# A state-space layer and a long-convolution layer on one core: a new order of all operations, planned with the DMA engines as one shared server, and larger blocks for x, q and the output

## The chip, the core and the metric

The kernel runs on one core of one Trainium2 chip. The metric is the device time of one execution in microseconds (us), lower is better. An execution varies: the kernel before took 229.8 to 240.2 us in its first three runs. A run more than 1.5% above the fastest of the same kernel in the same set is called slow and left out of ratios. A ratio here is the mean time of one kernel's fast runs over the mean time of the other kernel's fast runs in the same rounds on the same chip, so it is not quite the ratio of the medians that are quoted beside it.

## The reference, cut to what matters

Two layers read different inputs and fill the two halves of one output, 2048 x 1280.

```python
def _A_ref(x, Lambda_re, Lambda_im, B_re, B_im, C_re, C_im, log_dt, Dskip):   # x: 1 x 2048 x 640
    Lam_bar = jnp.exp(jnp.exp(log_dt) * Lam)
    Bu = einsum("bld,pd->blp", x, ((Lam_bar - 1.0) / Lam)[:, None] * Bmat)
    for t in range(L): h = Lam_bar * h + Bu[:, t, :]       # linear recurrence, 640 complex states
    y = 2.0 * einsum("blp,dp->bld", hseq, Cmat).real + x * Dskip

def _B_ref(q, k, v, shift_k, ssm_k, ssm_D):                # 1 x 2048 x 640 each
    kv = (k convolved with 4 taps shift_k) * v
    y = irfft(rfft(kv padded) * rfft(ssm_k padded)) + kv * ssm_D   # convolution of length 2048
    return q * y

return concatenate([a, b], axis=-1)
```

The kernel turns both into matmuls: the recurrence is done in blocks, the long convolution as a Fourier transform in two steps (`s1`, `s2`, the product, inverse steps `i2`, `i1`), for five groups of 128 channels.

## The kernel before: what the change and the argument touch

About 720 operations are declared with what they read and write. A text, ORDER, lists them by name, with the engine as a suffix where there is a choice (A ScalarE, D VectorE, G GpSimd, S SyncE). The kernel walks through the list and puts each operation on its engine's queue. Each engine does its queue strictly in order, so **the order decides what an engine waits for**.

```python
ORDER = """
ld_ldt ld_lre J0 consts J1 nrow ld_lim nrowf w0 xna pidx Dm0 w1 Dm1/G xnb hst1/S c4 B00 w2 bc zero par mk E0 ...
... zt2 s1h31 st_32/G e1h30/A ... d01_9 i120 cm30 ... py0_02 ob20 ...
... zt4 py1_21 i110 ey_21/D i131 ob10 ...
"""                                                       # cut: the rest of 720 names

def f_nrow():                                             # the seven powers of the sets, one iota each
    for i, n in enumerate(self.set_n):
        g.iota(nrow[:, i, :], pattern=[[0, 10]], base=n, channel_multiplier=0)

# the filter of group G, 512 KB (hst), and ssm_D (Dm), about 1 KB; dtap adds D to the filter's tap 0
op(f"hst{G}", {"SP": 0.4, "POOL": 1.2}, lambda e: self.eng[e].dma_start(
    out=self.S4(st)[:, 0:2048].rearrange("p (b t) -> p b t", b=16),
    in_=self.B_ssm_k[c0:c0 + 128, :].rearrange("(b c) (a t) -> (c a) b t", c=8, t=128)), ...)
op(f"dtap{G}", {"POOL": 0.2, "DVE": 0.1}, lambda e: self.eng[e].tensor_tensor(
    out=self.S4(st)[:, 0:2048:128], in0=self.S4(st)[:, 0:2048:128], in1=self.Dm[:, 16 * G:16 * G + 16], op=ALU.add), ...)

# B is loaded by four transposing loads from SyncE (B00, B01, B10, B11)
nc.sync.dma_start_transpose(out=self.BT[:, :, u, 320 * h:320 * h + 320], in_=ap[320 * h:320 * h + 320, :].rearrange(...))

# between the inverse steps: 1 MB from SBUF to SBUF, transposed (zt); i1 then reads Zt
op(f"zt{G}", {"SP": 5.0}, lambda e: nc.sync.dma_start_transpose(
    out=self.S8(Zt)[:].rearrange("p (b n) -> p b n", b=32), in_=self.S8(Zs)[:].rearrange("p (b n) -> p b n", b=32)), ...)
```

## Time and profile before

| | before |
|---|---|
| median of 3 runs | 232.91 us (229.82 to 240.19) |
| profiled span, TensorE busy | 230.8, 195.7 |
| TensorE idle | 35.1 |
| VectorE, ScalarE, GpSimd busy | 180.8, 140.7, 44.1 |

The span runs from the first to the last instruction. Where TensorE is the bound, what an order can win is TensorE's idle time plus what a throttled clock costs; the prediction below shows the lines and adds them up stage by stage.

### The profile page before, as it was taken

How to read it: one execution, taken by the hardware profiler on the slowest of the kernel's cores; microseconds unless marked ns; L12 is line 12 of the kernel's file. 1: busy time of each engine (PE TensorE's matmuls, PEld its weight loads, DVE VectorE, ACT ScalarE, POOL GpSimd, SP SyncE). 2: the span in 40 equal slices, each digit the busy share in tenths (PEclk: the TensorE clock that was granted, in tenths of full speed). 3: DMA queues.
4: the chain of work that ended last, by engine and by line, in shares of the span. 5: the costliest groups of instructions: out<-in, count | busy, mean ns of one | idle time of the engine just before them, and what ended most of it. 6: DMA issues, size and time to landing. Idle time of an engine off the chain costs nothing. (4 is left out here: it accounts for less than half of the span.)

```text
span 230.8 us, 8736 instructions
## 1 busy us (share of the span) xinstructions
PE 195.7 (85%) x3947; PEld 137.3 (59%) x3947; DVE 180.8 (78%) x279; ACT 140.7 (61%) x166; POOL 44.1 (19%) x67
## 2 busy tenths in 40 slices
PE   0619996979999999997659999659999999999953
PEld 0507443657456665645458776346777877777752
DVE  7699999859958799997546999915779899965641
ACT  3846928958556998778526795704267677852000
POOL 8288441600000020210200001002220003001600
PEclk9976999999999999999988999958999999999999
DMA  5999998997723079699968019990895482339966
GB/s 169 188 224 200 167 189 192 169 164 156 86 94 91 6 163 89 136 218 217 254 108 159 0 55 211 193 181 29 163 158 138 148 185 60 100 81 188 235 164 119
DMA packets 85407, 33.74 MB, mean 146 GB/s; under 512 B 81466, under 2 KB 82746, under 8 KB 85370
## 3 DMA queue, kind: packets, MB, share of 16 engines
q1 hardware_dynamic: 82972, 25.37, 61.0%
q0 software_dynamic: 2368, 7.81, 15.1%
q8 instruction: 30, 0.49, 0.9%
q14 instruction: 7, 0.06, 0.1%
q10 hardware_dynamic: 30, 0.00, 0.0%
HBM read 9.19 MB, written 7.86 MB: 74 GB/s over the span
## 5 line engine op out<-in xcount | busy, mean ns | idle before, releaser
L331 ACT CAST s<-ps 128x1024 bf16<-128x1024 f32 x81 | 78.4, 1020 | 26.0 <-PE ps L1002 12.9
L751 PE MATMUL ps<-xT,BC 128*64 128x512 bf16 x400 | 47.4, 381 | 0.2 <-ACT s L331 0.2
L899 PE MATMUL ps<-BC,hb 128*128 128x320 bf16 x240 | 38.1, 307 | 1.9 <-issue 1.7
L751 PEld LDWEIGHTS <-BC 128*64 128x64 bf16 x400 | 21.5, 110 | 18.0 <-issue 2.0
L1002 PE MATMUL ps<-R,s 64*64 64x128 bf16 x1280 | 24.7, 234 | 8.4 <-DVE s L924 4.3
L899 PEld LDWEIGHTS <-hb 128*128 128x128 bf16 x240 | 22.6, 100 | 12.4 <-issue 2.4
L1002 PEld LDWEIGHTS <-s 64*64 64x64 bf16 x1280 | 21.5, 118 | 13.0 <-issue 6.5
L333 DVE CAST s<-ps 128x1024 bf16<-128x1024 f32 x19 | 22.8, 1220 | 6.0 <-PE ps L1002 4.4
L856 DVE TENSOR_TENSOR hb<-ps,hb 128x512 bf16<-128x512 f32 x30 | 19.6, 684 | 9.3 <-PE ps L852 9.3
L1061 DVE TENSOR_TENSOR s<-s,s 128x1024 bf16<-128x1024 bf16 (+1 forms) x30 | 25.2, 866 | 1.0 <-PE ps L1002 0.3
L331 ACT CAST yo<-ps 128x640 bf16<-128x640 f32 x11 | 7.6, 691 | 28.8 <-PE ps L903 19.3
L1038 PE MATMUL ps<-s,Wre 128*64 128x128 bf16 x320 | 21.1, 221 | 0.4 <-issue 0.2
L1038 PE MATMUL ps<-s,Wim 128*64 128x128 bf16 x320 | 20.7, 219 | 0.0
L977 DVE TENSOR_TENSOR s<-s,s 128x2048 bf16<-128x2048 bf16 x15 | 19.3, 1290 | 1.2 <-ACT s L969 0.8
L1132 PE MATMUL ps<-Ct,s 128*64 128x64 bf16 x640 | 12.6, 201 | 8.8 <-DMA s<-s 6.9
L1038 PEld LDWEIGHTS <-Wre 128*64 128x64 bf16 x320 | 18.0, 110 | 2.8 <-issue 1.2
L1139 DVE TENSOR_TENSOR s<-ps,s 128x1024 bf16<-128x1024 f32 x10 | 12.1, 1222 | 9.0 <-PE ps L1132 6.6
L1038 PEld LDWEIGHTS <-Wim 128*64 128x64 bf16 x320 | 18.1, 110 | 0.9 <-issue 0.4
L331 ACT CAST hb<-ps 128x768 bf16<-128x768 f32 x17 | 13.5, 798 | 8.0 <-PE ps L751 8.0
L1132 PEld LDWEIGHTS <-s 128*64 128x64 bf16 x640 | 11.7, 117 | 10.1 <-DMA s<-s 7.6
L912 POOL DMA_DIRECT2D out_dram<-yo x6 | 3.4, 573 | 72.5 <-ACT yo L331 37.3
L1061 DVE TENSOR_TENSOR s<-s 128x1024 bf16<-128x1024 bf16 x20 | 13.8, 688 | 0.3
(161 smaller groups left out, 296.3 us busy)
## 6 DMA issues: line engine op xcount, KB each, us to landing
kvd<-s SPq DMA_DIRECT2D x4, 512.0 KB, 3.3
out_dram<-yo SPq DMA_DIRECT2D x10, 160.0 KB, 4.5
s<-in_B_ssm_k_dram POOLq DMA_DIRECT2D x3, 512.0 KB, 6.5
s<-kvd POOLq DMA_DIRECT2D x3, 512.0 KB, 7.6
s<-in_B_q_dram POOLq DMA_DIRECT2D x6, 256.0 KB, 8.0
out_dram<-s POOLq DMA_DIRECT2D x6, 256.0 KB, 5.6
s<-in_B_ssm_k_dram SPq DMA_DIRECT2D x2, 512.0 KB, 7.0
s<-kvd SPq DMA_DIRECT2D x2, 512.0 KB, 4.8
```

Of the source, the lines that this page charges most:

```text
L331: self.nc.scalar.copy(out=out, in_=in_)
L333: self.eng[e].tensor_copy(out=out, in_=in_)
L751: nc.tensor.matmul(P[64 * ri:64 * ri + 64, b, :], lhsT=self.BT[:, k, ri, 64 * j:64 * j + 64], rhs=self.xT[:, k, hf, 2 * b:2 * b + 2, :].re ...
L856: v.tensor_tensor(out=hv(r), in0=self.P(p2)[:, 0, :].rearrange("p (h m) -> p h m", h=2), in1=hv(r), op=ALU.add)
L899: nc.tensor.matmul(P[:, part, 0:320], lhsT=hap(j), rhs=self.CT[:, j, c0:c0 + 320], start=(j == 0), stop=False)
L912: self.eng[e].dma_start(out=self.o2[r0:r0 + 2033:16, 0:D], in_=self.yo[yo.slot][:])
L977: op(f"ca{j}{G}{h}", {"DVE": dve_tt(W_)}, lambda e, c=c, tt=tt: v.tensor_tensor(out=c(), in0=c(), in1=tt(), op=ALU.add), r=[f"tm{G}{h}"], ...
L1002: nc.tensor.matmul(P[64 * ri:64 * ri + 64, r, 128 * b4:128 * b4 + 128], lhsT=d[64 * r:64 * r + 64, 4 * qd + b4, a0, :], rhs=self.R[64 * r: ...
L1038: nc.tensor.matmul(P[64 * pi:64 * pi + 64, ri, 128 * k4:128 * k4 + 128], lhsT=W[:, kp, pi, :], rhs=A[:, kp + 16 * pi, :], start=True, stop ...
L1061: v.tensor_tensor(out=o, in0=a, in1=b, op=op_)
L1132: nc.tensor.matmul(P[64 * ah:64 * ah + 64, b // 8, 64 * (b % 8):64 * (b % 8) + 64], lhsT=Z[:, 16 * h + b, 64 * ri:64 * ri + 64], rhs=self. ...
L1139: v.tensor_tensor(out=o, in0=self.P(pt)[:].rearrange("p s (b a c) -> p a (s b) c", b=8, a=16), in1=o, op=ALU.mult)
```

## The change

**Intent.** The program that had found the old order counted a transposing load as time of SyncE and almost none of the DMA engines'; the new one lets it take its turn in the one server that all transfers share, and counts GpSimd work of 0.25 us or more as a slowdown of VectorE beside it. These model constants run on no engine. What runs is different in these ways:

- the order is new throughout, and most stores and loads are issued by SyncE instead of GpSimd;
- the first half of x arrives in two pieces of 640 KB, not 960 and 320, and is transposed and copied by piece;
- q and the output of the second layer move as one transfer of 128-row blocks each, not two of 64-row blocks (the columns of Ct, the matrix of the last inverse step, are reordered to match);
- the second product of the spectrum (pQ) is one operation with a reversed block view instead of two;
- `nrow` is filled by two iotas instead of seven, and one small copy (F16) is gone.

```diff
-ld_ldt ld_lre J0 consts J1 nrow ld_lim nrowf w0 xna pidx Dm0 w1 Dm1/G xnb hst1/S c4 B00 w2 bc zero par mk E0 ld_sk/G p0 dtb R
+xn0 ld_lre J0 consts nrow xn1 J1 zero ld_ldt E0 pidx w0 ld_lim c4 nrowf hst1/G B00 E1 wi0 kz0/D bc kz1/G px00 wm0 px02 ex00/A
+px04 Dm0 w1 ex02/A Dm1/G px10 ex04/A par px12 ex10/A px14 p0 ex14/D B01 dtb ex12/A p1 fi w2 nrho ph mk rn k0 R dtap1/G Ct
 ... (the rest of the order is replaced as well)
-            for i, n in enumerate(self.set_n):
-                g.iota(nrow[:, i, :], pattern=[[0, 10]], base=n, channel_multiplier=0)
+            g.iota(nrow[:, 0:3, :], pattern=[[1, 3], [0, 10]], base=1, channel_multiplier=0)
+            g.iota(nrow[:, 3:7, :], pattern=[[4, 4], [0, 10]], base=4, channel_multiplier=0)
 ...
-        op("xna", ... in_=xr[:, 0:6, :]) ; op("xnb", ... in_=xr[:, 6:8, :])          # 960 KB, 320 KB
+        for b in range(2): op(f"xn{b}", ... in_=xs[:, 0, b])                          # 640 KB each
 ...
-                    tt(X(0), X(0), H(1), ALU.mult)
-                    tt(X(1), X(1), H(0), ALU.mult)
+                    o = self.S4(xs)[:, 0:2048].rearrange("p (r n) -> p r n", r=2)
+                    tt(o, o, self.S8(Hf)[:, 2048 * h:2048 * h + 2048].rearrange("p (r n) -> p r n", r=2)[:, ::-1, :], ALU.mult)
 ...
-            for hh in range(2):
-                self.eng[e].dma_start(out=self.S4(q)[64 * hh:64 * hh + 64, 0:2048]..., in_=q2[1024 * hh:1024 * hh + 1024, c0:c0 + 128]...)
+        self.eng[e].dma_start(out=self.S4(q)[:, 0:2048].rearrange("p (a c) -> p a c", a=16),
+                              in_=q2[:, c0:c0 + 128].rearrange("(a p) c -> p a c", p=128))
```

## The prediction

> **What bounds the kernel now.** I read the page first (busy time, the 40 slices), then busy time by stage, cut at the points where TensorE stops and starts, then the waits of TensorE, the chain that ended last, and the order of time in the first 26 us.
>
> ```profile
> PE 195.7 (85%) x3947; PEld 137.3 (59%) x3947; DVE 180.8 (78%) x279; ACT 140.7 (61%) x166; POOL 44.1 (19%) x67
> ...
> PE   0619996979999999997659999659999999999953
> ...
> PEclk9976999999999999999988999958999999999999
> DMA  5999998997723079699968019990895482339966
> ```
>
> TensorE is the bound wherever it has work. The figures to look at are the low digits of the PE row: the start, slices 18 to 21, slices 25 and 26, the end. The clock row drops just after each.
>
> ```profile
> 0.00:17.33 17.33, 4.77 (x43) 4.00 (x43) 13.84 (x50) 10.09 (x16) 11.29 (x29) 0.91 0.99 194
> ...
> 36.25:50.00 13.75, 10.67 (x276) 7.54 (x276) 11.58 (x32) 11.91 (x15) 4.97 (x6) 1.00 1.01 180
> ...
> 100.00:121.00 21.00, 14.43 (x472) 10.42 (x474) 13.66 (x22) 13.07 (x19) 2.13 (x3) 0.97 1.07 200
> ...
> 140.00:152.30 12.30, 7.60 (x164) 4.76 (x161) 9.42 (x13) 6.34 (x6) 0.95 (x3) 0.93 1.27 178
> ...
> 205.00:227.20 22.20, 19.22 (x481) 15.27 (x479) 9.91 (x10) 3.63 (x4) 4.48 (x6) 1.00 0.92 189
> 227.20:230.80 3.60, 0.00 (x0) 0.00 (x0) 0.82 (x1) 0.00 (x0) 0.00 (x0) 1.00 0.39 88
> ```
>
> Columns: stretch, length, busy PE, PEld, DVE, ACT, POOL, clock, DMA share, GB/s. Length less PE busy is TensorE's idle time: 12.56, 3.08, 6.57, 4.70, 2.98 and 3.60, together 33.5 us; the stretches left out hold 1.6. So 35.1 of 230.8 us can be won by order, the rest only by less work. In the stretches with long gaps the DMA share is about 1: the transfers queue.
>
> ```profile
> PE ps L1132 <- DMA s<-s: 6.9, 4, 4.3
> PE ps L1002 <- DVE s L924: 4.3, 1, 4.3
> ...
> 140.93 11.35 DMA s<-s
> 152.27 0.04 issue
> 152.32 1.92 PE ps L1132 x64
> ```
>
> L1132 is the last inverse step (i1); it waits for the 1 MB SBUF transpose Zs to Zt (zt). The last lines are the chain: zt of group 2 is issued at 140.93 and takes 11.35 us to land, TensorE having run out of other work at 148.
>
> ```profile
> 12.71 2.33 POOL L674 TENSOR_TENSOR s<-s,F 128x1280 int32<-128x1280 int32 x1
> 12.77 2.32 DVE L503 CAST ss<-cs 64x70 bf16<-64x70 f32 x1
> 15.11 0.21 DVE L504 TENSOR_SCALAR ss<-sn 64x70 bf16<-64x70 f32 x1
> ...
> 17.14 3.67 DVE L516 TENSOR_TENSOR M<-E,ss 128x640 bf16<-128x640 bf16 x2
> ```
>
> A 70-element cast takes 2.32 us beside a GpSimd product of 2.33; its twin without GpSimd work takes 0.20. Two set products take 3.67 beside GpSimd, one alone 0.81. This delay holds L924 (dtap1), so the first transform starts at 17.33.
>
> **What the Trainium skill says.** "SBUF — State Buffer", Who interferes with whom: GpSimd and VectorE share a port pair as an exclusive lock, for VectorE's two-port modes and for two SBUF inputs against a GpSimd read. The trace agrees (2.32 against 0.20). "DMA: Bandwidth & Descriptors", Issuing engines are not separate DMA queues: work started from any engine interleaves on the same 16 engines. The trace agrees: zt takes 9.4 to 11.3 us to land while its issue takes 4.9 to 7.0, with other queues active. "ScalarE: Activation LUTs", What ACT_TABLE_LOAD costs: 1283 ns, plus a drain of about 1380. The trace shows four loads of 1.283 us each; it does not show the drain (the instruction before a load ends 0.02 us before it). "TensorE: Matmul & The Clock Gate", HAM oscillation: an idle gap of over about 3.4 us throttles the array. The trace agrees: after the gap that ends at 152.3 the granted clock of 150 to 160 is 0.66, and ten L899 matmuls take 2.67 us instead of 1.36.
>
> **The change, part by part.** The arithmetic on TensorE is the same: 40 transposing matmuls of x in another grouping, everything else equal. Most of the diff is planner constants, which run on no engine; they only gave the new order.
>
> *Start.* x comes in two 640 KB pieces, both ahead of the parameter loads. Before, 960 KB issued at 1.55 landed 5.1 us later and all of x at 7.5; now the first piece should land near 5.2, the second near 7.2. But the new order puts the copies of x on ScalarE (1.02 us for 1024 columns, about 0.6 for 512) ahead of the exp of dt, and the small cosines (w2) between the two exps. ScalarE by hand: copies 5.9 to 8.5 and to 9.5, table load and exp 11.0, copy 12.0, cosines with a load 14.4, so the R table (0.76 on VectorE) at 15.2; exp again with two loads 17.4, trig 18.2. That is five loads for four, +1.28. Four first transforms at 15.2 fill the four PSUM slots, and the slots free from 19.1 on. So the first projection (L751, 20.89 before) starts near 19.3. Sets: ss at 19.4 without the 2.1 us stretch; three VectorE products beside five on GpSimd, about 1.8 each as in the 3.67 above, end near 24.8. TensorE reaches m1 of the first unit at 24.8 to 25.3 with five half-units behind it, where the old kernel had four at 25.33: about 0.5 + 1.15 = **1.6 us won**.
>
> *25 to 50 us.* VectorE lost about 2 us more here to GpSimd issues and products (L971 1.64 for 0.74 + L977 2.16 for 1.23 near 28 to 31), and TensorE waited 2.12 for its copy of hb at 36. The new order issues k/v stores and small loads from SyncE and has 23 projection halves in a row before the first group-0 transform. 3.08 idle should become 1: **2.1 won**.
>
> *The two i1 stages.* The new order still lets zt of 1 and 0 wait for the C buffers, then gives TensorE 7 corrections (0.3), 4 s2 (0.46) and two output halves pairs (1.6 each), with VectorE's seven additions of 0.68 pacing the corrections: about 10 us ahead of i11, against a landing of 10 to 11; and about 5 more ahead of i10, whose transpose follows 6 us later. I count 1 to 2 us for landing and 3 for VectorE's pace, 4.5. Group 2's zt now has nearly 40 us of other work ahead of i12, so its 4.7 go. 6.57 + 4.70 − 4.5 = **6.8 won**.
>
> *Clock.* The slow stretches after these two gaps cost L1132 0.8, L899 1.3, and L1002 at 120.55 1.4 (97 matmuls in 2.87, where 128 took 1.98): 3.5. With most of the gaps gone, **2.5 won**. The cold start stays.
>
> *Tail.* From zt4's issue: i130, i131, i121 (1.1 each) and four half outputs (1.6 each), 9.7 us, against a landing of 9.4 to 10.8, so a stall of up to 1 and up to 1 for zt3; then i14 2.3, two blocks 6.4, copy 0.8, store 2.8. Idle 2.98 + 3.60 becomes 5.6: **1.0 won**.
>
> *Smaller parts.* q and output as one transfer for two: the bytes and 256-byte runs are the same; GpSimd pays 1.19 (the price of a 512 KB issue there) for 1.69. pQ as one 2048 product for two of 1024: 10 × (2 × 0.688 − 1.221) = 1.55 us of VectorE, mostly beside TensorE. F16's copy 0.64, nrow 5 iotas of 0.15 on GpSimd: off the path. I add nothing for these.
>
> Sum won: 1.6 + 2.1 + 6.8 + 2.5 + 1.0 = 14.0, a span of 216.8. A list order of 720 operations in one queue per engine always meets waits that were not planned; I give back 30%, 4.2: span 221.0. Time exceeded span by 2.0 before (232.81 against 230.8), so **223.0 us**.
>
> **The rivals.** (1) *The wait moves.* The DMA engines are already 77% busy (61.0 + 15.1 + 0.9) and the same bytes must pass in less time, with 15 of 16 x-side stores, all q loads and four kvl now queued in order on SyncE, which also issues the transposes (up to 7 us each). A zt or kvl held there holds TensorE. For it: SyncE's transposes sit behind earlier ones. Against it: before, SyncE's own waits were mostly for its inputs, and 50 to 100 us had only 0.62 of DMA share. It would leave 228 to 231. (2) *The ScalarE chain at the start costs more than won*: five loads, x copies first, R later; if R comes at 18 the start loses 2 us and the time is about 226. (3) *VectorE becomes the bound*: 180.8 us of work in a 221 span is 82%; a reversed block view in pQ that lost its fast mode would add 10 × about 1 us. The profile can't tell; time 227. (4) *All gains arrive*, 216.8 + 2.0 = 219, or less if the clock never drops.
>
> **Range and chances.** Centre 223.0. All gains and half a microsecond of luck per stage: 217. Rival 1 or 3: up to 229.5. Two per cent under 232.91 is 228.3: only rival 1 at strength or two rivals together reach it. The old runs spread from 229.8 to 240.2, which blurs the line. Faster 0.82, same 0.15, slower 0.03.
>
> **What would show it.** Right: TensorE idle falls to about 25 us, L1132's wait for s from 6.9 to 3 or less, no clock under 0.8 after 30 us, the first L751 near 19.3, five table loads, L1061 at 2048 × 20 with 1.22 each. Wrong: a long wait of L1002 for kvd, of L1132 late, or of SyncE's queue on a store ahead of a transpose; a first L751 after 21; L1061 over 2 us; a DMA share of 1 with TensorE idle in a new place.

## The result and the profile after

The changed kernel took **218.35 us** (median of 4 runs, 216.99 to 221.79), the kernel before in the same rounds 236.55 (229.82 to 245.06; two of its four runs fast); the ratio of the fast runs is 0.942 (95% interval 0.925 to 0.959). The profiled run of that set was a slow one (221.79), so the lines below are from the control run described further on (the same kernel again, all four runs fast, 218.19 to 218.52).

The page of the control run: busy time, the 40 slices, the granted clock.

```profile
PE 193.3 (89%) x3947; PEld 136.3 (63%) x3947; DVE 173.7 (80%) x264; ACT 149.4 (69%) x173; POOL 29.2 (13%) x41
...
PE   0839999999999899999599999997999989999892
...
PEclk9999999999999999999999999999999999999999
```

Against the row of before, the two holes in the middle (slices 19 to 21, 26 and 27, counted from 1) have become one 5 and one 7, and the row of the granted clock never falls below nine tenths. TensorE is busy 193.3 us for the same 3947 matmuls that took 195.7. The slow start is still there, though this row does not show it: the 128 matmuls of the first transform take 3.63 us, as in the kernel before, and 128 of the same form take 1.98 at 44.65.

Busy time by stage of the control run; the columns are those that the prediction explains.

```profile
0.00:14.35 14.35, 4.73 (x43) 4.25 (x44) 10.22 (x49) 9.01 (x12) 5.13 (x19) 1.00 0.98 208
...
36.00:50.00 14.00, 13.54 (x240) 8.12 (x240) 11.96 (x23) 12.23 (x16) 8.37 (x7) 1.00 1.02 188
50.00:75.00 25.00, 23.00 (x572) 15.88 (x568) 20.93 (x34) 20.24 (x23) 0.72 (x2) 1.00 0.95 163
...
100.00:121.00 21.00, 17.82 (x414) 11.60 (x414) 17.98 (x33) 15.63 (x18) 0.00 (x0) 1.00 0.75 128
...
212.30:216.40 4.10, 0.18 (x4) 0.00 (x0) 0.00 (x0) 0.69 (x1) 0.00 (x0) 0.99 0.27 91
```

Length less PE busy is again TensorE's idle time: 9.62 at the start (12.56 before), 0.46 from 36 to 50 (3.08), 3.18 from 100 to 121 (6.57). The whole is 216.4 - 193.3 = 23.1 us instead of 35.1.

The waits of TensorE in the control run, the two lines that answer to those shown of before (L1147 is the old L1132, L1019 the old L1002):

```profile
PE ps L1019 <- POOL s L941: 4.6, 2, 4.1
...
PE ps L1147 <- DMA s<-s: 0.9, 1, 0.9
```

The last inverse step waits 0.9 us (once) for its transposed data instead of 6.9 (four waits). The first transform still waits 4.1 us at the start. The order of time shows for what (start, us, engine, line; in brackets the idle time before and what ended it):

```profile
1.83 1.31 POOL L938 DMA_DIRECT2D s<-in_B_ssm_k_dram  x1
...
5.62 4.38 SPq L743 DMA_TRANSPOSE BC<-in_A_B_im_dram  x1
...
6.80 0.93 POOL L369 DMA_DIRECT2D Dm<-in_B_ssm_D_dram  x1 [2.53 <-DVE rowa L571]
...
12.92 0.76 DVE L605 TENSOR_TENSOR R<-vs,mk 128x256 bf16<-128x256 f32 x2
...
14.03 0.26 POOL L941 TENSOR_TENSOR s<-s,Dm 128x16 bf16<-128x16 bf16 x1 [1.61 <-DMA Dm<-in_B_ssm_D_dram]
...
14.35 3.63 PE L1019 MATMUL ps<-R,s 64*64 64x128 bf16 x128 [4.11 <-POOL s L941]
...
17.09 0.19 DVE L522 CAST ss<-cs 64x70 bf16<-64x70 f32 x1
...
17.91 5.80 PE L768 MATMUL ps<-xT,BC 128*64 128x512 bf16 x50
```

The first filter's load (512 KB) is issued by GpSimd at 1.83 and, by the view of that line, lands 8.8 us later, at 10.6. The load of D, about 1 KB, is issued at 6.80 behind the transposing loads of B and lands 7.1 us later, at 13.9; the first transform waits for it, not for the rotation table R, which is ready at 13.7. The cast of 70 elements takes 0.19 us where it took 2.32 before: no GpSimd product runs beside it.

### The profile page after: what moved, and what is told of

The parts are those of the page before. It is cut to its first block, busy times and chain, and to the rows that moved or that the text cites. A ratio compares the mean times of both kernels' runs of the same rounds, so it can differ in the third digit from the quotient of the medians.

```text
span 219.7 us, 8702 instructions
## 1 busy us (share of the span) xinstructions
PE 195.0 (89%) x3947; PEld 137.3 (63%) x3947; DVE 174.8 (80%) x264; ACT 149.4 (68%) x173; POOL 29.0 (13%) x41
## 4 chain that ended last, share of the span: by engine, by line
PE 68%; DMA 13%; DVE 7%; ACT 6%; issue 4%; POOL 0%; POOLq 0%; DVEq 0%; ACTq 0%; SPq 0%
PE ps L768 19%; PE ps L916 18%; PE ps L1019 8%; PE ps L1055 6%; DMA s<-kvd 5%; DMA s<-s 5%; PE ps L1111 4%; ACT s L350 4%; DMA Dm<-in_B_ssm_D_dram 3%; PE ps L1147 3%; PE ps L869 3%; PE ps L776 2%; DVE s L352 2%; PE ps L920 2%; ACT BC L350 2%
## 5 line engine op out<-in xcount | busy, mean ns | idle before, releaser
L350 ACT CAST s<-ps 128x1024 bf16<-128x1024 f32 x83 | 79.9, 1025 | 21.2 <-PE ps L1019 9.7
L916 PE MATMUL ps<-BC,hb 128*128 128x320 bf16 x240 | 36.4, 299 | 0.0
L768 PEld LDWEIGHTS <-BC 128*64 128x64 bf16 x400 | 22.8, 112 | 20.4 <-issue 4.0
L1019 PE MATMUL ps<-R,s 64*64 64x128 bf16 x1280 | 23.8, 227 | 10.8 <-issue 5.4
L350 ACT CAST yo<-ps 128x640 bf16<-128x640 f32 x14 | 9.7, 693 | 32.0 <-PE ps L920 22.6
L1019 PEld LDWEIGHTS <-s 64*64 64x64 bf16 x1280 | 20.8, 113 | 14.8 <-issue 9.1
L352 DVE CAST s<-ps 128x1024 bf16<-128x1024 f32 x17 | 20.5, 1219 | 7.2 <-PE ps L1019 5.1
L1078 DVE TENSOR_TENSOR s<-s,s 128x2048 bf16<-128x2048 bf16 x20 | 24.4, 1222 | 0.8 <-ACT s L350 0.3
L994 DVE TENSOR_TENSOR s<-s,s 128x2048 bf16<-128x2048 bf16 x15 | 20.3, 1354 | 0.4
L986 ACT ACTIVATE s<-s,sk 128x2048 bf16<-128x2048 bf16 x9 | 18.1, 2014 | 3.0 <-DVE sk L660 2.5
L1147 PE MATMUL ps<-Ct,s 128*64 128x64 bf16 x640 | 11.6, 197 | 0.9 <-DMA s<-s 0.9
L1147 PEld LDWEIGHTS <-s 128*64 128x64 bf16 x640 | 10.7, 113 | 2.3 <-DMA s<-s 1.1
```

The source lines that it names most:

```text
L350: self.nc.scalar.copy(out=out, in_=in_)
L352: self.eng[e].tensor_copy(out=out, in_=in_)
L768: nc.tensor.matmul(P[64 * ri:64 * ri + 64, b, :], lhsT=self.BT[:, k, ri, 64 * j:64 * j + 64], rhs=self.xT[:, k, hf, 2 * b:2 * b + 2, :].re ...
L916: nc.tensor.matmul(P[:, part, 0:320], lhsT=hap(j), rhs=self.CT[:, j, c0:c0 + 320], start=(j == 0), stop=False)
L986: nc.scalar.activation(out=out, in_=k(j), func=ACT.Copy, scale=self.sk[:, G, j:j + 1])
L994: op(f"ca{j}{G}{h}", {"DVE": dve_tt(W_)}, lambda e, c=c, tt=tt: v.tensor_tensor(out=c(), in0=c(), in1=tt(), op=ALU.add), r=[f"tm{G}{h}"], ...
```

## The experiments

All kernels gave a correct result. "Before" varies from set to set, so kernels are compared within a set of runs on one chip: in the first set (old_order_new_code, order_only, new_start, old_start) the one fast run of before took 232.03 us; in the second (after_again, order_only_dm, dm_early, early_start) three took 234.6 to 235.1; in the third (nrow_old, nrow_old_hst1_first, zt2_early, dm_mid), on another chip, three took 236.2 to 239.4.

### Which part is worth what: code without order, order without code

**old_order_new_code**: all the small parts and the two pieces of x, in the old order.

```diff
-xn0 ld_lre J0 consts nrow xn1 J1 zero ld_ldt E0 ...
+ld_ldt ld_lre J0 consts J1 nrow ld_lim nrowf w0 xn0 pidx Dm0 w1 Dm1/G xn1 hst1/S ...   # the order of before, x by pieces
```

> Everything of the change except the order: q and output as one transfer, the two pieces of x, pQ as one product, two iotas, no F16 copy, run in the old order with the old engine choices. Theory (the order did it): within 1% of before, 230 to 234, and L1132's counterpart still waits 6 to 7 us for zt. Rival (the small parts did it): under 225.

Measured: median 230.43 us (227.11 to 233.5); two fast runs, mean 228.3, against 232.03. That is 1.6% less, so the theory's 1% was missed by a little and the rival's 225 by more; it rests on one fast run of before. The profile still has the wait that the new order removes:

```profile
PE ps L1150 <- DMA s<-s: 7.1, 4, 2.9
```

**order_only**: the new order, with seven iotas for nrow, q and output in halves (and the old columns of Ct that go with them), pQ as two products.

```diff
+            for i, n in enumerate(self.set_n): g.iota(nrow[:, i, :], pattern=[[0, 10]], base=n, channel_multiplier=0)
+                    tt(X(0), X(0), H(1), ALU.mult); tt(X(1), X(1), H(0), ALU.mult)
+            for hh in range(2): self.eng[e].dma_start(...64-row halves of q and of the output...)
```

> The new order and x in two pieces, but q and output again as two 64-row transfers each, pQ as two products, nrow as seven iotas. Theory (order): 217 to 221, at most 1% over the changed kernel. Rival (the one-transfer q and output freed the DMA engines or SyncE): 225 or more.

Measured: 228.18 us (226.8 to 230.38), fast mean 227.7. The expectation missed by about 7 us, and the time lies in the rival's range. Its span was 225.2, with TensorE idle 30.8 us; 16.1 of these lie in the first 25 us, where the control has 9.6. So 6.4 of the 7.7 us of extra idle time are at the start: the first transform began at 20.94 instead of 14.35, again waiting for the filter and D (`L941`), with the filter issued at 2.25 and landing 13.7 us later. The small parts, for which the prediction had added nothing, were worth something after all, and the place pointed to the start. Side by side: 232.0 before, 228.3 with the code alone, 227.7 with the order alone, 218.4 with both (the control, from the second set). Neither alone wins more than 4.3 us and both win 13.6, so a good part of the gain needs both.

### Which half of the order: two hybrids

**new_start**: the new order up to the first transform of filter 0 (about 44 us in the new kernel), then the old sequence of what is left. **old_start**: the old sequence up to about 54 us, then the new.

```diff
 # new_start
-... e3_6_0/A s1h00 e3_5_0/A s1h01 e1h00/A ci0 ...
+... e3_6_0/A ci0 ci1 dn0_9_0 dn1_9_0 e1_9_0/D m1_9_0 s1h00 e3_9_0/D s1h01 ...
 # old_start
-xn0 ld_lre J0 consts nrow xn1 ...
+ld_ldt ld_lre J0 consts J1 nrow ... e3_8_0/D set_8_1/G dn0_7_0 dn1_7_0 e1_7_0/D m1_7_0 ...
```

> Code of the changed kernel; new order up to the first transform of group 0's filter (about 44 us), then the remaining operations in the old order. Theory (most of the gain is in the later i1 stages, 9 of 14 us): the start brings 4 to 5 us, so about 227 to 229, with the zt waits of 4 us and more still there. Rival (the start is the main thing): 222 or less.

> Code of the changed kernel; old order up to s2k01 (about 54 us), then the rest in the new order. Theory: 221 to 224, no zt wait over 1 us, first dense transform at 17 us as before. Rival (start is the main thing): 226 or more.

Measured: new_start 234.35 us (231.84 to 235.25, all fast), old_start 228.4 (226.89 to 229.28, all fast), the kernel before 232.03. Both theories missed: new_start lies beyond its rival's range too, old_start in its rival's (226 or more). new_start has its first transform at 14.40 and yet gains nothing; the old sequence behind it keeps its gaps, and its clock row falls to 0.6 to 0.7 after them:

```profile
PE ps L1150 <- DMA s<-s: 4.6, 3, 2.3
PE ps L1150 <- issue: 4.5, 2, 3.9
```

old_start has no such wait, but new ones at the seam (3.6 for a kv load, 3.5 us counted as issue). **The parts of this order do not add up.** A likely reason, argued and not shown, is that each half was planned for the state of queues and buffers that its own other half leaves. A hybrid tells which waits belong to which half; its time does not tell what that half is worth. Why new_start is even slower than the old order with the new code (228.3) is not explained in full.

### What happens at the start

**after_again** is the unchanged new kernel, as a control.

> The changed kernel itself, as the control on this chip: 217 to 220, ratio to before about 0.94.

Measured: 218.41 us (218.19 to 218.52), ratio 0.930 (0.927 to 0.933).

Three tries followed from the wait for D. **order_only_dm** and **dm_early** put the load of D ahead of the filter's, in order_only and in the new kernel; **early_start** goes further and brings the parameters and exps ahead of the copies of x.

```diff
 # dm_early (the same move in order_only_dm)
-xn0 ld_lre J0 consts nrow xn1 J1 zero ld_ldt E0 pidx w0 ld_lim c4 nrowf hst1/G B00 ... px04 Dm0 w1 ex02/A Dm1/G
+xn0 ld_lre J0 consts Dm0 nrow xn1 J1 zero ld_ldt E0 pidx w0 ld_lim c4 Dm1/G nrowf hst1/G B00 ... px04 w1 ex02/A
 # early_start
+xn0 ld_lre J0 consts xn1 J1 Dm0 ld_ldt pidx w0 c4 E0 ld_lim Dm1/G nrow zero hst1/G B00 w1 par nrowf p0 dtb p1 nrho rn fi ph
+w2 px00 mk R px02 ex00/A E1 px04 ex02/D trig ex04/A ...
```

> order_only with the small load of Dm and its memset moved ahead of the first filter load on GpSimd. In order_only the first transform waited 10.2 us, at 20.94, for this load, which took 13 us to land. Theory (the small parts' apparent worth is mostly this one wait): first transform at 13.5 to 14.5 and a time of 220 to 222. Rival (q, output and pQ are worth it themselves): 225 or more.

> The changed kernel with the same move alone. There the load lands at 13.9 and R is ready at 13.73, so theory: first transform at about 13.8 instead of 14.34, time 0 to 0.6 us less (ratio to the changed kernel 0.997 to 1.0). Rival (the load's landing decides between faster and slower executions): a narrower spread and more than 1 us less.

> The changed kernel with its first part in another order: Dm early; both exps directly behind the parameter loads, then all sines, then the copies of x, so two table loads fewer on ScalarE; the index work ahead of everything on VectorE; two half-units more on TensorE ahead of the first m1. Theory: R by 9 to 10 us, first transform at 10 to 11.5, first projection at 13 to 15 instead of 17.9, time 214 to 217. Rival (what follows is bound by VectorE and ScalarE, and gives the start back as waits for copies): 218 or more with TensorE waiting for copies between 20 and 60 us.

Measured: order_only_dm 224.78 (220.71 to 226.75), its profiled run slow; dm_early 225.41 (222.52 to 229.15), ratio 0.953, **slower than the control by 2.4% by the fast means** (223.7, two runs, over 218.4); early_start 223.09 (222.72 to 224.09), ratio 0.951. In the new kernel the theory that the load of D is what holds the start fell: with D ahead of it the filter was issued at 2.87 in dm_early and landed 17.5 us later, and the first transform began at 21.34. In order_only the same move helped: its one fast run took 220.71 against a mean of 227.7, which meets the expected 220 to 222, and in its profiled (slow) run D landed at 10.9 instead of 20.3 and the first transform began at 16.95 instead of 20.94, not at the expected 13.5 to 14.5. early_start lies in its rival's range (218 or more), but TensorE waited only 0.4 us for copies between 20 and 60 us, so not for the rival's reason. The first transform waits for whichever of the two lands last: the filter in these three kernels, D in all others of the table below.

That gave a new theory: GpSimd's filter load races the transposing loads of B. The Trainium skill, "DMA: Bandwidth & Descriptors", Queues, rings and completion order, says that each DMA engine takes turns between its queues at the grain of a packet. So a load under way must share with one that comes in; if the filter's load is issued a little later it has more company, and five iotas of 0.1 us ahead of it would matter. Two runs tested this directly.

**nrow_old**: the new kernel with only the seven iotas restored. **nrow_old_hst1_first**: the same, with the filter's load ahead of them.

```diff
 # both
-            g.iota(nrow[:, 0:3, :], pattern=[[1, 3], [0, 10]], base=1, channel_multiplier=0)
-            g.iota(nrow[:, 3:7, :], pattern=[[4, 4], [0, 10]], base=4, channel_multiplier=0)
+            for i, n in enumerate(self.set_n):
+                g.iota(nrow[:, i, :], pattern=[[0, 10]], base=n, channel_multiplier=0)
 # nrow_old_hst1_first also
-xn0 ld_lre J0 consts nrow xn1 J1 zero ld_ldt E0 pidx w0 ld_lim c4 nrowf hst1/G B00
+xn0 ld_lre J0 consts hst1/G nrow xn1 J1 zero ld_ldt E0 pidx w0 ld_lim c4 nrowf B00
```

> The kernel after with one thing undone: the seven small fills of the table of powers are seven GpSimd iotas again instead of two. Theory (the start is a race of loads): five more iotas of about 0.1 us stand ahead of the 512 KB load of the first filter on GpSimd, so it is issued at about 2.25 us instead of 1.83, is overtaken by the transposes of B and lands only at about 20; the first transform on TensorE starts at 20 to 21 instead of 14.3 and the time is 224 to 227 us. Rival (it was the q and output transfers in halves and the two y products that the run of the new order alone lost by): first transform still near 14.3, 218 to 219.5 us.

> The same seven iotas, but the filter's load stands ahead of them in GpSimd's order, so it is issued before 1.83 us. Theory (the moment of the issue decides, not the iotas): the first transform is back at 14 to 15 us and the time at 217 to 220. Rival (the iotas cost by themselves, through what waits for the table of powers or through VectorE's slower operations beside them): as long as the run with seven iotas ahead, 222 or more.

Measured: nrow_old 225.27 us (222.75 to 227.32), fast mean 223.3; nrow_old_hst1_first 219.78 (218.57 to 220.86), fast mean 219.8. The order of time of nrow_old (from a run of 227.32 us, called slow; its fast runs were not profiled):

```profile
2.25 1.31 POOL L938 DMA_DIRECT2D s<-in_B_ssm_k_dram  x1
...
5.18 9.71 SPq L743 DMA_TRANSPOSE BC<-in_A_B_im_dram  x1
...
6.57 0.93 POOL L369 DMA_DIRECT2D Dm<-in_B_ssm_D_dram  x1 [1.88 <-DVE rowa L571]
...
22.55 0.26 POOL L941 TENSOR_TENSOR s<-s,Dm 128x16 bf16<-128x16 bf16 x1 [8.71 <-DMA Dm<-in_B_ssm_D_dram]
```

and of nrow_old_hst1_first:

```profile
1.40 1.31 POOL L941 DMA_DIRECT2D s<-in_B_ssm_k_dram  x1 [0.33 <-issue]
...
5.82 4.64 SPq L746 DMA_TRANSPOSE BC<-in_A_B_im_dram  x1
...
14.77 3.63 PE L1022 MATMUL ps<-R,s 64*64 64x128 bf16 x128 [4.99 <-POOL s L944]
```

nrow_old_hst1_first met its expectation. nrow_old went the way that the theory said, not exactly by its numbers: the median lies in the expected 224 to 227 and the fast mean just under, the filter landed at 17.4 and not about 20, and the first transform began at 22.87 and not at 20 to 21. Five iotas ahead of the load delay its issue by 0.42 us and, in the profiled run, its landing from 10.6 to about 17.4 and the first transform by 8 us; the same iotas behind the load cost nothing that shows (219.8 against 218.4 in another set). By the fast means of this set the 0.42 us are worth 3.5 us of the whole (5.5 by the medians, which hold slow runs). The profiled run is 8.75 us longer than that of nrow_old_hst1_first, so it made up nothing; whether the filter landed sooner in the fast runs is not known. The profile of order_only, from a fast run, has the late landing too (13.7 us after an issue at 2.25). SyncE's queue shows the loss from the other side: the second transposing load of B is held 9.71 us at its issue instead of 4.38.

**dm_mid** tried to use this: the filter's load stays at 1.83, the load of D follows at once, and the chain to R goes ahead of two copies of x.

```diff
-... J1 zero ld_ldt E0 pidx w0 ld_lim c4 nrowf hst1/G B00 ... px04 Dm0 w1 ex02/A Dm1/G px10 ex04/A par px12 ex10/A px14 p0 ex14/D B01 dtb
-ex12/A p1 fi w2 nrho ph mk rn k0 R dtap1/G Ct s1h10 trig scol
+... J1 Dm0 zero ld_ldt E0 pidx w0 ld_lim c4 nrowf hst1/G Dm1/G B00 ... px04 w1 ex02/A px10 ex04/A par px12 ex10/A px14 p0 B01 dtb
+p1 nrho rn fi ex12/A ph ex14/D w2 mk k0 R dtap1/G trig Ct s1h10 scol
```

> A try to beat both. The filter's load stays at 1.83 us; the tiny load of D follows it at once on GpSimd (3.1 us instead of 7.1), ahead of the transposes of B that held it till 13.9; and on ScalarE and VectorE the chain to the rotation (par, dt, rho, phase, R) goes ahead of two copies of x. Theory: the filter lands by 10 to 12, so the first transform starts at about 12.5 to 13 instead of 14.3 and the first projection near 16.3 instead of 17.9: 216.5 to 217.5 us. Rival (hst1 itself lands only at about 13.5, or the 1 us that the issue costs GpSimd holds up the filter's tables): no gain, 218 to 220.

Measured: 222.44 us (220.84 to 225.37), fast mean 221.9. It lost by more than its rival had said (218 to 220), and its profile limits the theory:

```profile
1.83 1.32 POOL L941 DMA_DIRECT2D s<-in_B_ssm_k_dram  x1
...
3.14 0.90 POOL L372 DMA_DIRECT2D Dm<-in_B_ssm_D_dram  x1
...
16.98 3.63 PE L1022 MATMUL ps<-R,s 64*64 64x128 bf16 x128 [7.20 <-POOL s L944]
```

The filter was issued at the same 1.83 as in the control, yet landed 13.6 us later, not 8.8. So the moment of the filter's issue is not all of it; a second GpSimd issue right behind it goes with a late landing too. All profiled runs with the new order's start or a variant of it, with the filter's and D's issue and landing and the first transform (the profiles of after, nrow_old, dm_early and order_only_dm are of slow runs):

| kernel | filter issued, landed after | D issued, landed after | first transform |
|---|---|---|---|
| nrow_old_hst1_first | 1.40, 8.3 | 7.87, 6.5 | 14.77 |
| after_again | 1.83, 8.8 | 6.80, 7.1 | 14.35 |
| after (the first set) | 1.83, 8.7 | 7.07, 6.8 | 14.34 |
| new_start | 1.83, 8.7 | 6.80, 7.1 | 14.40 |
| zt2_early | 1.83, 8.7 | 6.80, 7.1 | 14.39 |
| dm_mid | 1.83, 13.6 | 3.14, 13.4 | 16.98 |
| order_only | 2.25, 13.7 | 6.58, 13.7 | 20.94 |
| nrow_old | 2.25, 15.2 | 6.57, 15.9 | 22.87 |
| dm_early | 2.87, 17.5 | 1.83, 10.0 | 21.34 |
| order_only_dm | 3.28, 13.2 | 2.24, 8.7 | 16.95 |
| early_start | 3.64, 12.2 | 2.33, 11.2 | 16.35 |

Shown: the filter lands within 8.8 us where it goes out by 1.83 with nothing else from GpSimd close behind, and after 12 to 17.5 us in every other case of this order (from SyncE, in the old orders, it took 9.0 to 9.8).

The traces also count packets by queue and window (`--dma --window`), which says more of how. The software queue carries what GpSimd issues (0.51 MB from 6 to 9 us in the control, the filter's size), the hardware queue what SyncE issues. Here is the software queue from 6 to 9 us, in after_again, nrow_old and dm_mid (packets, MB, share of the DMA engines' time):

```profile
q0 software_dynamic: 137, 0.51, 68.1%
...
q0 software_dynamic: 32, 0.13, 55.6%
...
q0 software_dynamic: 159, 0.51, 71.3%
```

| 9 to 16 us | after_again | nrow_old | dm_mid |
|---|---|---|---|
| software queue, packets and MB | 52, 0.00 | 104, 0.37 | 30, 0.00 |
| hardware queue, packets and MB | 5919, 1.33 | 1166, 0.29 | 1749, 0.44 |
| DMA share, GB/s in all | 1.32, 191 | 1.22, 95 | 1.33, 63 |

In the control the filter goes through before the bulk of the transposing loads; in nrow_old the two move side by side, which agrees with the page cited above, and both are slow: the engines are about as busy and move half as much (112 GB/s in order_only, from a fast run). In dm_mid the filter's data went through as in the control (packet by packet in the trace, its last 4096 bytes end at 8.9 us, against 8.7 in the control and 16.7 in nrow_old). What came late there is the signal of its landing (15.4) and the small load of D (16.5), and beside the last 30 small packets of GpSimd the transposing loads moved a third of what they moved in the control. So dm_mid does not speak against the race; it shows that a landing can be signalled 6.5 us after the data. Open: why the two kinds of load are so slow beside each other, and what part D has in dm_mid, which also moved other things (two copies of x and the parameter chain). Not tested either is whether VectorE's work holds up what GpSimd does for its loads; the issue of the filter itself took 1.31 to 1.32 us in the control, nrow_old, order_only and dm_mid alike.

### What the long transposing load is worth

**zt2_early**: the new kernel with the two last inverse steps of group 2 and their products moved back to shortly behind the issue of their transposing load.

```diff
-... s1h42 st_01/S s1h43 e1h41/A pP31 ...
+... s1h42 st_01/S s1h43 i120 ob20 i121 ob21 e1h41/A pP31 ...
-... st_10/S i120 e343/D ... ob31 py1_23 ob20 ob3/G i121 ey_23/A py0_21 st_23/S ob21 py1_21 ...
+... st_10/S e343/D ... ob31 py1_23 ob3/G ey_23/A py0_21 st_23/S py1_21 ...
```

> The kernel after, with the two inverse transforms of slice 2 (the ones that read the transposed state zt2) and their copies moved back to right behind the transform of filter 4, a few us after the transposing load of zt2 is issued; nothing else moved. Theory of the prediction (6.8 us of the gain is these waits, and a transposing load takes about 10 us): TensorE waits 3 to 4.5 us for it, the tail loses two stages of filler, and the time is 4 to 7 us longer, 222 to 225. Rival (hybrids have shown that waits taken away in one place come back in another, so a wait put in is absorbed as well): within 1 us of 218.3.

Measured: 227.26 us (224.53 to 229.29), fast mean 225.6, against 219.8 of nrow_old_hst1_first, the kernel of the same set that is nearest to the control: 5.8 us more. The expectation of the prediction's theory (4 to 7 more) held; the rival (absorbed within 1 us) fell. Its waits, a line of its order of time, and its clock row:

```profile
PE ps L1150 <- DMA s<-s: 4.0, 3, 2.6
...
PE ps L1150 <- DVE s L1157: 1.4, 1, 1.4
```

```profile
171.58 1.61 PE L1150 MATMUL ps<-Ct,s 128*64 128x64 bf16 x64 [2.57 <-DMA s<-s]
```

```profile
PEclk9958999999999999999999999999998599999999
```

TensorE waits 2.6 us for the load and 1.4 for VectorE behind it, and the clock drops to 0.77 of full speed from 165 to 180 us: 64 matmuls take 1.61 where they take 1.20 in the control. This agrees with the Trainium skill, "TensorE: Matmul & The Clock Gate", HAM oscillation, in kind; that the drop came with a wait of 2.6 us, shorter than the 3.4 us that the page gives, is what the run shows (what else counted is not known). The low clock in slices 3 and 4 is not counted: it is in the profiles of some kernels on both chips and not in the control's, while the first 128 matmuls take 3.63 us in zt2_early, in the control and in the kernel before alike.

No experiment beat the changed kernel. It stays the best measured; nrow_old_hst1_first is equal to it within what these runs can tell.

## Why the prediction was right, and where it was off

The verdict (faster by over 2%) was right and the time was inside the range; the centre, 223.0, was 4.65 us too high. The idle time of the control run, with the clock's share, can be set beside the terms of the sum:

| term | predicted won | measured |
|---|---|---|
| start | 1.6 | 12.56 - 9.62 = 2.9 |
| 25 to 50 us | 2.1 | 3.08 - 0.46 = 2.6 |
| the two i1 stages | 6.8 | 6.57 + 4.70 - 3.18 - 0 = 8.1 |
| tail | 1.0 | 2.98 + 3.60 - 4.83 = 1.75 |
| clock (TensorE busy) | 2.5 | 195.7 - 193.3 = 2.4 |
| given back | 4.2 | 5.04 - 1.6 = 3.4 |
| net, span | 9.8 | 230.8 - 216.4 = 14.4 |

The tail's 4.83 is the idle time from 180 us to the end; 5.04 is what TensorE idles in all other stretches of the control (2.00 of it from 50 to 75 us, 1.09 from 150 to 180), against 1.6 before. The split is by stretch, not by step: the i1 steps now run between 123 and 143 us, and what is left from 100 to 121 is other waits, the longest 1.39 and 0.85 before first transforms. Were these counted as given back, the i1 stages would have won more and the give-back would be larger; the net is the same.

- **The bound and the mechanism were right.** The waits for the transposing load fell from 6.9 us (four) to 0.9 (one), and zt2_early shows, by bringing group 2's back, that it was worth about 6 us with its clock and what follows. The clock's term fell where it was said to: the busy time of L899 went from 38.1 to 36.4 us, of L1132 from 12.6 to 11.6, of L1002 from 24.7 to 23.8. (The prediction's "slices 18 to 21" are 19 to 21, counted from 1.)
- **The give-back existed and, split in this way, was nearly the right size**: 3.4 instead of 4.2. So the fourth rival, all gains arrive at 219, has the right number for another reason. What was mis-sized were the gains: 17.8 us instead of 14.0, most at the start (1.3 short) and in the i1 stages (1.3 short). There the prediction had kept 4.5 us of waits ahead of i11 and i10, for loads that land after 10 to 11 us and for VectorE's pace; the five loads landed after 7.2 to 9.5 us (9.4 to 11.3 before), and TensorE idles 1.2 us in all from 121 to 150, where i11 and i10 run.
- **The start was right in its effect and wrong in its cause.** The prediction counted "five loads for four" on ScalarE and let the rotation table decide at 15.2. The trace has four table loads: the first one, at 1.39, already serves the exp of dt at 9.78, as no load stands between. R was ready at 13.7, so the second rival (R at 18) did not come, and the tiny load of D, which the prediction does not mention, decided at 14.3. The first projection came at 17.91, not 19.3.
- **"I add nothing for these" was the step that failed.** It counted the seven iotas by their duration. nrow_old shows what they hold back: 3.5 us by fast means in this order. order_only lost 9.3 us (fast means of two sets, so about); its profile has 6.4 us more idle time at the start. In the old order the small parts were worth 3.7 us (228.3 against one fast run of before). What q, the output and pQ are worth was not measured alone and stays open.
- **The reversed view kept its speed**, which settles that part of the third rival: 20 products of 2048, ten of them reversed, took 1.211 to 1.226 us each. Nor did VectorE become the bound: it is busy 80% of the span and TensorE 89%.

```profile
L1078 DVE TENSOR_TENSOR s<-s,s 128x2048 bf16<-128x2048 bf16 x20 | 24.4, 1221 | 1.1 <-ACT s L350 0.3 <-PE ps L1111 0.2
```

- **The first rival, a wait that moves to SyncE's queue, did not come**, though the queue got 15 of 16 stores; the clock stayed full after 30 us, as predicted. VectorE's busy time fell from 180.8 to 173.7, GpSimd's from 44.1 to 29.2.

## What to carry to other kernels

In the first microseconds, judge a small instruction by what stands behind it in its queue: 0.4 us of iotas ahead of the load that everything waits for cost 3.5 us, and nothing that shows when it stood behind. Look at which load the DMA engines take first, and not only at when it lands: from 9 to 16 us, two loads side by side moved half of what the same engines moved in the control. Put several other pieces of work between a long transposing load and its reader (here about 10 us of it), as the wait cost twice here, once in time and once in clock. Don't read the value of half an order from a hybrid: the hybrids took 228.4 and 234.35 us where the whole order took 218.4.

## What the Trainium skill lacked or had wrong

- "DMA: Bandwidth & Descriptors", Issuing engines are not separate DMA queues: it says that all transfers interleave, and that choosing the issuer saves only issue time. It lacks what interleaving can do to one of them: a 512 KB load from GpSimd landed 8.8 us after an issue at 1.83, and 15.2 us after an issue at 2.25, with the same transposing loads behind it; side by side, all loads together moved 95 GB/s from 9 to 16 us instead of 191.
- The same page has no figure for a 1 KB load behind transposing loads: 7.1 us in the control, 15.9 in nrow_old.
- "ScalarE: Activation LUTs", What ACT_TABLE_LOAD costs: 1283 ns per load agrees (four of 1.283 us); the drain of about 1380 ns that it adds shows in no trace here (in the control the load at 11.21 starts 0.02 us after the activation before it and ends 0.02 us before the next).
- "Vector Engine (DVE) Microarchitecture Reference", Performance modes — why throughput varies by op and dtype: it lists the streaming of an operand with a negative step as not measured. A step of -1 over two blocks of 1024, contiguous inside, ran at 1.221 us for 2048 elements a row; before, two forward halves of 1024 took 0.688 each.
